# Attention with soft experts on one core: x transposed into the products' bank, the second head's maxima transposed at the block's end, another order of the start and of the late weights' tiles

## The chip, the core and the metric

The kernel runs on one core of a Trainium2 chip. The metric is the device time of one execution in microseconds. The core has a matrix engine (TensorE, PE; its weight loads run in a queue of their own, PEld), three engines for elementwise work (VectorE: DVE, ScalarE: ACT, GpSimd: POOL), and SyncE (SP), which here only issues DMA transfers. Every engine takes its instructions in program order; between engines semaphores order the work.

## The reference

Attention with a causal mask over 8 batches of 12 heads, then a soft mixture of experts over the whole output. All is float32.

```
q, k, v: 8 x 12 x 448 x 64
scores = (q @ k^T) / sqrt(64), above the diagonal -1e9
attn = softmax(scores);  o = attn @ v
x = o as 3584 rows x 768
logits = x @ phi                       # phi 768 x 32: 8 experts x 4 slots
d = softmax(logits over rows)          # dispatch weights
slots = d^T @ x                        # 32 x 768
out_e = relu(slots_e @ w1_e) @ w2_e    # w1 768 x 1024, w2 1024 x 768, 8 experts
c = softmax(logits over slots)         # combine weights
result = c @ out
```

## The kernel before, in words

**Blocks.** The 96 heads are taken in 48 pairs; `block(p)` handles pair p, with heads a = 2p and a + 1, six blocks to a batch. The blocks overlap: block p computes the first part of the scores of the heads a + 2 and a + 3 and finishes those of a and a + 1.

**Scores.** q and k are split in a rounded part (`qd`, `ks`, cast by ACT) and the rest (POOL's subtractions `sub_q`, `sub_k`; `r2_`, named `r20` and `r21`, holds q's rest). `scores1_all` puts the mask and the product of the rounded parts in one of three score tiles `s_`, each two PSUM banks. `max_keys` is DVE's maximum over keys: one pass over the tile with a transposition (1.25 us), then two small ones, into `r_`. `max_row` transposes these maxima on PE (`rt`) and reduces them once more on DVE (`mr`, negated). `max_spread`, a select on POOL, writes them into r2_, from where `scores2` adds them, with the products of the rests, to the scores by matmul. `exps` is ACT's exponential (`pt`).

**Products.** `attv` and `attv3` multiply pt by v (`va`) into `po`, a PSUM bank for both heads. The v tile has a column of ones, so po holds the sums of the exponentials too. `norm(p, 0..2)` divides by them on DVE: sums (`sm`), reciprocals, then x, in one tensor operation and two small ones. `xtrans(p)` transposes x on PE (`xt`, four matmuls), and ACT copies it out (`xts`).

**PSUM.** The three score tiles take six banks, po one, and the last one is the buffer "m" that `misc` gives out in turn: to rt, to xt and to filler matmuls (`warm`).

**The mixture.** With xt of two blocks, `next_logits` adds a third of a batch's logits (PE into a score tile, DVE into `lt`). Which work stands at the end of block p follows from m6 = p % 6: at 2, 4 and 0 logits, at 0 also the batch's maximum (`logits_b`), at 1 the dispatch weights' transposes (`logits_e`), at 3 and 5 a `dispatch`, eight matmuls of x with the dispatch weights, added to `si` on DVE. The last block carries the second dispatch of the batch before the last. After block 47 come the last logits, and the experts, whose weights are 64 pieces of 768 KB, some loaded two at a time.

**Loads.** SP issues all loads of q, k, v and weights in one queue, in program order; one that waits holds all behind it. w0 to w22 have space of their own and are loaded in every second block (`load_w`). The others, w23 to w34, called the late loads here, lie over tiles of attention, in the order in which these were allocated (the pools raw, `fix`, `wk`, `moe`); each waits for the last reader of what it overwrites. `hw`, the next load, waits for a matmul of the first expert.

**Order.** Nothing is scheduled by the compiler: the helper `_InOrder.call` (L65, the line of all instructions in the profile) keeps the order in which the code is written. `START` holds the counts of filler matmuls in the prologue. `later` is a list of small settings on POOL (mk, run_m, run_z, si, sid, srep), of which blocks 1 to 6 issue two each.

Of the kernel before, what the change touches and what calls it, by code (L numbers as in the profile page):

```python
# [17 lines left out]
P = 128  # L18
# [17 lines left out]
HT = 2  # L36
WN, PAD = 1536, 168
WARM = (2, 5, 2, 3, 3)
START = (8, 3, 5, 1, 18, 9)


FILL = 9
# [38 lines left out]
def attention_soft_moe(ctx: ExitStack, tc: tile.TileContext, qk, va, phi, w1, w2, out):  # L81
# [16 lines left out]

    x_, va_, pt_ = [None] * XB, [None, None], [None, None]
    qd_, ks_ = [fix.tile([P, 2, S], F32R, name="qd0")], [fix.tile([P, 2 * S + KP], F32R, name="ks0")]  # L100
    x_[1] = fix.tile([P, NCH, 3 * P], F32, name="x1")
    qd_.append(fix.tile([P, 2, S], F32R, name="qd1"))
    r_ = [fix.tile([P, RW], F32, name=f"r{i}") for i in range(2)]
    ks_.append(fix.tile([P, 2 * S + KP], F32R, name="ks1"))
    r2_ = [fix.tile([P, 2, S], F32R, name="r20")]
    va_[0] = fix.tile([P, NCH, 2, VC], F32, name="va0")

    k2_ = fix.tile([P, 2 * S + KP], F32R, name="k2")
    r2_.append(fix.tile([P, 2, S], F32R, name="r21"))
    pt_[0] = wk.tile([P, 1024], F32, name="pt0")  # L110
# [80 lines left out]
    nc.gpsimd.affine_select(out=tri, in_=tri, compare_op=ALU.is_ge, fill=NEG,  # L191
                            base=0, pattern=[[1, P]], channel_multiplier=-1)

    pob = ps_1.tile([P, NQ * VC], F32, name="po")
    po2 = pob.rearrange("p (a b)->p a b", b=VC)
    po0 = po2[:, 0:NCH]
    identb = const.tile([P, P], BF16, name="identb")

# [11 lines left out]
    def misc(name):  # L210
        return ps_1.tile([P, 512], F32, tag="m", name=name)
# [37 lines left out]
    def scores1(i, part):  # L249
        if i >= NHD:  # L250
            return
        p, h = divmod(i, 2)
        ks, qd = ks_[p % NR], qd_[p % NR]
        if ("s", i) not in st:
            st["s", i] = s_[i % 3]
            st["open"] = set()
        s = st["s", i]

        bank = part in ("c12", "k1", "k2")
        start = bank not in st["open"]  # L260
        st["open"].add(bank)
        if part[0] == "k":
            c = int(part[1])
            o, w, m = S * h + P * c, S - CQ0[c], min(P, S - P * c + KP)
            nc.tensor.matmul(s[0:m, SCOL[c]:SCOL[c] + w], ks[:, o:o + m],
                             qd[:, h, CQ0[c]:S], start=start, stop=False, skip_group_check=True)
            return
        if part == "c12":
            o = s[:, SC1:SC1 + 2 * SC2].rearrange("p (a n) -> p a n", n=SC2)[:, :, 0:P]
            mask = tri.unsqueeze(1).to_broadcast([P, 2, P])  # L270
        else:
            w = P if part == "c0" else S - 3 * P
            o, mask = s[:, SCOL[int(part[1])]:SCOL[int(part[1])] + w], tri[:, 0:w]
        nc.tensor.matmul(o, identb, mask, start=start, stop=False, skip_group_check=True)
# [26 lines left out]
    def max_row(i, k):  # L301
        if i >= NHD:
            return
        if k == 0:
            st["rt", i] = misc(f"rt{i}")
            nc.tensor.transpose(out=st["rt", i][0:RW - RF, 0:P], in_=r_[i % 2][:, RF:RW], identity=ident)
        else:
            mr = st["mr", i] = wk.tile([NQB, 32], F32, tag="mr", name=f"mr{i}", bufs=2)
            nc.vector.tensor_reduce(out=mr, in_=st.pop(("rt", i))[0:NQB, 0:P].rearrange("p (g t)->p t g", g=4),
                                    axis=AX.X, op=ALU.max, negate=True)  # L310
# [12 lines left out]
    def scores2(i, cs):  # L323
        if i >= NHD:
            return
        p, h = divmod(i, 2)
        s = st["s", i]
        k2, r2 = k2_, r2_[p % NR]
        for c in cs:
            o, w, m = S * h + P * c, S - CQ0[c], min(P, S - P * c + KP)  # L330
# [55 lines left out]

    def xtrans(p):
        x = st.pop(("x", p))
        pt = misc(f"xt{p}")
        for c in range(NCH):  # L390
            nc.tensor.transpose(out=pt[:, P * c:P * c + P], in_=x[:, c], identity=ident)
        xt = st["xt", p] = xtp.tile([P, 512], F32, tag="xt", name=f"xts{p}", bufs=XT)
        nc.scalar.activation(out=xt, in_=pt, func=AF.Copy)

    def logits_a(b, js, g, first=True, last=True):

# [52 lines left out]
        logits_a(b, (j, j + 1), m[:, 0:P])  # L449
        logits_t(j, m[:, 0:P])  # L450

    warm(START[0], a=x_[1][:, NCH - 1, 0:AW].bitcast(BF16))
    h0, h1 = slice(0, 1), slice(1, 2)
    cast_k(0, h0)
    cast_q(0, h0)
    cast_k(0, h1)
    for hs in (h0, h1):
        sub_k(0, hs, nc.vector)
    sub_q(0, h0)
    scores1_all(0)  # L460
    warm(START[1])

    cast_q(0, h1)
    sub_q(0, h1)
    scores1_all(1)
    warm(START[2])
    copy_k2(0, h0)
    cast_k(1, h0)
    cast_k(1, h1)
    cast_q(1, h0)  # L470
    copy_k2(0, h1)
    cast_q(1, h1)

    for i, k in ((0, 0), (0, 1), (0, 2), (1, 0)):
        max_keys(i, k)
    sub_k(1, h0)
    max_row(0, 0)
    warm(START[5], pob[:, 0:2 * P])
    max_row(0, 1)
    max_spread(0)  # L480
    for k in (1, 2):
        max_keys(1, k)
    sub_k(1, h1, nc.vector)
    cast_k(2)
# [5 lines left out]
    for hf in range(2):  # L490
        nc.sync.dma_start(out=phis[hf], in_=phi[:, 3 * hf:3 * hf + 3])
# [17 lines left out]

    later += [lambda: nc.gpsimd.tensor_copy(out=srep, in_=sid.unsqueeze(1).to_broadcast([P, 4, NSLOT]))]  # L510

    def block(p):
        a, b = 2 * p, p // 6 - 1
        last, m6 = p == NPAIR - 1, p % 6
        if p + 1 < NPAIR:
            loads_v(p + 1, nc.sync if p + 1 < NPAIR - 1 else nc.scalar)
        if p % 2 and p // 2 < RES:
            load_w(p // 2)
        load_qk(p + 3, 0)

        max_row(a + 1, 0)
        max_row(a + 1, 1)
        max_spread(a + 1)
        if p:
            norm(p - 1, 2)
        else:
            sub_q(1)
        scores2(a, range(NCH))
        exps(a)
        scores1_all(a + 2)  # L530
        for k in range(3):
            max_keys(a + 2, k)
        cast_q(p + 2)
        if p:
            xtrans(p - 1)
        scores2(a + 1, range(NCH))
        exps(a + 1)
        scores1_all(a + 3)
        max_keys(a + 3, 0)
        sub_k(p + 2)  # L540
        load_qk(p + 4, 1)
        sub_q(p + 2)
# [6 lines left out]
        max_spread(a + 2)  # L549
        for k in (1, 2):  # L550
# [354 lines left out]
```

## Time and profile before

| | us |
|---|---|
| median of 3 runs (lowest to highest) | 431.97 (431.29 to 433.31) |
| the profiled execution | 431.9 |
| its span in the trace | 430.2 |
| PE busy / DVE busy / ACT busy / POOL busy | 378.6 / 296.9 / 284.1 / 263.6 |
| first products of block 0 | 17.05 |
| products of block 46 | 320.38 |
| issue of hw | 337.98 |
| last matmuls of the experts | 402.52 |

The span runs from the first to the last event of the trace; 1.7 us of the execution lie outside it. In the rows below, the columns are start, duration, engine, line, operation, output<-inputs, partitions x elements and count; brackets give how long the engine stood idle before, and which event ended that. PE's ends overlap, since its matmuls are pipelined.

### The profile page before, as it was taken

How to read it: one execution, taken by the hardware profiler on the slowest of the kernel's cores; microseconds unless marked ns; L12 is line 12 of the kernel's file. 1: busy time of each engine (PE TensorE's matmuls, PEld its weight loads, DVE VectorE, ACT ScalarE, POOL GpSimd, SP SyncE). 2: the span in 40 equal slices, each digit the busy share in tenths (PEclk: the TensorE clock that was granted, in tenths of full speed). 3: DMA queues.
4: the chain of work that ended last, by engine and by line, in shares of the span. 5: the costliest groups of instructions: out<-in, count | busy, mean ns of one | idle time of the engine just before them, and what ended most of it. 6: DMA issues, size and time to landing. Idle time of an engine off the chain costs nothing.

```text
span 430.2 us, 14170 instructions
## 1 busy us (share of the span) xinstructions
PE 378.6 (88%) x5763; PEld 288.9 (67%) x5763; DVE 296.9 (69%) x817; ACT 284.1 (66%) x400; POOL 263.6 (61%) x215
## 2 busy tenths in 40 slices
PE   6799899999999999999999999999998998968740
PEld 3587778777877777787788777777876644533430
DVE  5777687787787877877877878778774575332440
ACT  5587788878877977888788779778863112422340
POOL 5798988878877978888788779787850000000000
PEclk9999999999999999999999999999999999999985
DMA  7668776777767787767777767876575999999998
GB/s 263 218 216 278 238 251 195 263 252 249 261 187 249 257 257 249 249 194 262 255 243 247 230 218 258 257 257 240 161 272 201 418 419 425 423 422 413 401 389 345
DMA packets 34481, 119.18 MB, mean 277 GB/s; under 512 B 3824, under 2 KB 8944, under 8 KB 32880
## 3 DMA queue, kind: packets, MB, share of 16 engines
q1 hardware_dynamic: 34272, 118.01, 77.9%
q8 instruction: 46, 0.75, 0.7%
q10 hardware_dynamic: 144, 0.27, 0.2%
q14 instruction: 19, 0.16, 0.1%
HBM read 107.25 MB, written 11.01 MB: 275 GB/s over the span
## 4 chain that ended last, share of the span: by engine, by line
PE 37%; DVE 27%; DMA 14%; POOL 8%; issue 5%; ACT 1%; DVEq 0%; POOLq 0%; SPq 0%
PE po L65 18%; DMA w<-in_w_dram 14%; DVE r L65 14%; PE s L65 11%; DVE x L65 7%; POOL r L65 5%; PE rt L65 2%; DVE mr L65 2%; POOL ks L65 2%; PE xt L65 1%; PE pp L65 1%; DVE lt L65 1%; PE hp L65 1%; PE e L65 1%; DVE si L65 1%
## 5 line engine op out<-in xcount | busy, mean ns | idle before, releaser
L65 ACT ACTIVATE pt<-s 128x1024 f32<-128x1024 f32 x96 | 98.4, 1025 | 56.5 <-PE s L65 38.1
L65 DVE TRANSPOSE_TENSOR_REDUCE r<-s 128x32 f32<-128x1024 f32 x96 | 120.0, 1250 | 12.5 <-PE s L65 10.3
L65 POOL TENSOR_TENSOR r<-qk,qd 64x896 fp32r<-64x896 f32 (+1 forms) x49 | 101.0, 2061 | 3.8 <-ACT qd L65 3.6
L65 POOL TENSOR_TENSOR ks<-qk,ks 64x896 fp32r<-64x896 f32 (+1 forms) x47 | 97.9, 2084 | 3.7
L65 PE MATMUL po<-va,pt 128*64 128x65 f32 x3040 | 99.4, 223 | 0.0
L65 PEld LDWEIGHTS po<-va,pt 128*64 128x64 f32 x3040 | 92.8, 138 | 5.8 <-issue 0.2
L65 POOL TENSOR_SCALAR_AFFINE_SELECT r<-mr 14x448 fp32r<-14x448 f32 x96 | 61.4, 640 | 52.4 <-DVE mr L65 47.0
L65 PE MATMUL s<-qd,ks 128*66 128x64 f32 (+3 forms) x384 | 79.2, 318 | 1.9 <-DVE ks L65 1.9
L65 PE MATMUL s<-r,k 128*128 128x448 f32 (+3 forms) x384 | 69.3, 302 | 5.1 <-POOL r L65 4.1
L65 PEld LDWEIGHTS s<-r,k 128*128 128x128 f32 (+1 forms) x384 | 58.6, 183 | 9.8 <-POOL r L65 8.3
L65 PEld LDWEIGHTS s<-qd,ks 128*128 128x128 f32 (+1 forms) x384 | 50.6, 184 | 2.1 <-DVE ks L65 2.1
L65 ACT ACTIVATE ks<-qk 128x896 fp32r<-128x896 f32 (+1 forms) x50 | 46.0, 922 | 6.5 <-DMA qk<-in_qk_dram 2.5
L65 ACT ACTIVATE qd<-qk 128x896 fp32r<-128x896 f32 (+1 forms) x50 | 45.8, 915 | 1.3 <-DMA qk<-in_qk_dram 1.3
L65 ACT ACTIVATE k<-ks 64x896 fp32r<-64x896 f32 (+1 forms) x49 | 45.8, 935 | 1.1
L65 PE MATMUL s<-tri,identb 128*128 128x128 bf16 (+2 forms) x288 | 43.2, 238 | 1.2
L65 PE MATMUL rt<-ident,r 128*76 128x128 f32 x96 | 27.7, 288 | 11.9 <-DVE r L65 11.8
L65 DVE TENSOR_REDUCE r<-r 128x16 f32<-128x32 f32 x192 | 33.7, 176 | 4.9
L65 PEld LDWEIGHTS rt<-ident,r 128*76 128x76 f32 x96 | 11.0, 115 | 38.9 <-issue 23.5
L65 PE MATMUL xt<-ident,x 128*128 128x128 f32 x188 | 31.7, 285 | 2.5 <-DVE x L65 2.5
L65 DVE TENSOR_SCALAR sm<-po 128x7 f32<-128x7 f32 (+1 forms) x48 | 7.9, 165 | 35.6 <-PE po L65 35.6
L65 PEld LDWEIGHTS xt<-ident,x 128*128 128x128 f32 x188 | 22.4, 140 | 11.5 <-PE s L65 4.6
L65 PEld LDWEIGHTS <-identb 128*128 128x128 bf16 x320 | 24.9, 100 | 5.5 <-issue 4.5
(137 smaller groups left out, 400.5 us busy)
## 6 DMA issues: line engine op xcount, KB each, us to landing
qk<-in_qk_dram SPq DMA_DIRECT2D x94, 448.0 KB, 4.5
w<-in_w_dram SPq DMA_DIRECT2D x43, 768.0 KB, 6.0
w<-in_w_dram SPq DMA_DIRECT2D x10, 1536.0 KB, 24.9
va<-in_va_dram SPq DMA_DIRECT2D x47, 260.0 KB, 3.5
out_dram<-ot SPq DMA_DIRECT2D x16, 384.0 KB, 6.7
out_dram<-ot SPq DMA_DIRECT2D x2, 1536.0 KB, 9.3
qk<-in_qk_dram SPq DMA_DIRECT2D x4, 224.0 KB, 3.3
hw<-in_w_dram SPq DMA_DIRECT2D x1, 768.0 KB, 12.1
```

The costliest lines, as they stand in the source:

```text
L65: return self._tc.keep_in_program_order(op(*args, **kwargs))
```

## The change

1. `xtrans` writes its four transposes into po's bank (now 512 columns) and not into the buffer "m", and ACT copies from there.
2. `max_row` and `max_spread` of the second head (a + 3) move from the start of the next block to the end of this one, right behind the products; 64 columns are transposed (`AW`) instead of 76.
3. The prologue: 14 filler matmuls in place of 44; head 0 is done alone first, without the `KP` = 2 extra columns of keys, which belong to head 1; `later` is issued at once, behind the first subtraction; one more subtraction on DVE and one more on POOL change places; block 0 takes over some of the casts and subtractions.
4. The `fix` tiles are allocated in another order, so the late loads lie over other tiles.
5. w22 is loaded in block 44 and not in block 45.
6. The dispatch of the last block moves to the end of block 46, into the second bank of its score tile.

```diff
-START = (8, 3, 5, 1, 18, 9)
+START = (8, 4, 2)
...
     qd_, ks_ = [fix.tile([P, 2, S], F32R, name="qd0")], [fix.tile([P, 2 * S + KP], F32R, name="ks0")]
+    r2_ = [fix.tile([P, 2, S], F32R, name="r20")]
+    qd_.append(fix.tile([P, 2, S], F32R, name="qd1"))
+    ks_.append(fix.tile([P, 2 * S + KP], F32R, name="ks1"))
+    va_[0] = fix.tile([P, NCH, 2, VC], F32, name="va0")
     x_[1] = fix.tile([P, NCH, 3 * P], F32, name="x1")
-    qd_.append(fix.tile([P, 2, S], F32R, name="qd1"))
     r_ = [fix.tile([P, RW], F32, name=f"r{i}") for i in range(2)]
-    ks_.append(fix.tile([P, 2 * S + KP], F32R, name="ks1"))
-    r2_ = [fix.tile([P, 2, S], F32R, name="r20")]
-    va_[0] = fix.tile([P, NCH, 2, VC], F32, name="va0")
...
-    pob = ps_1.tile([P, NQ * VC], F32, name="po")
+    pob = ps_1.tile([P, 512], F32, name="po")
...
-            o, w, m = S * h + P * c, S - CQ0[c], min(P, S - P * c + KP)
+            o, w, m = S * h + P * c, S - CQ0[c], min(P, S - P * c + (KP if i else 0))
...
-            nc.tensor.transpose(out=st["rt", i][0:RW - RF, 0:P], in_=r_[i % 2][:, RF:RW], identity=ident)
+            nc.tensor.transpose(out=st["rt", i][0:w, 0:P], in_=r_[i % 2][:, RF:RF + w], identity=ident)
...
     def xtrans(p):
         x = st.pop(("x", p))
-        pt = misc(f"xt{p}")
         for c in range(NCH):
-            nc.tensor.transpose(out=pt[:, P * c:P * c + P], in_=x[:, c], identity=ident)
+            nc.tensor.transpose(out=pob[:, P * c:P * c + P], in_=x[:, c], identity=ident)
         xt = st["xt", p] = xtp.tile([P, 512], F32, tag="xt", name=f"xts{p}", bufs=XT)
-        nc.scalar.activation(out=xt, in_=pt, func=AF.Copy)
+        nc.scalar.activation(out=xt, in_=pob, func=AF.Copy)
...
+    sub_k(0, h0, nc.vector)
+    sub_q(0, h0)
+    for f in later:
+        f()
+    scores1_all(0)
+    warm(START[1])
...
-        if p % 2 and p // 2 < RES:
+        if p % 2 and p // 2 < RES - 1 or p == 2 * RES - 2:
             load_w(p // 2)
...
-        max_row(a + 1, 0)
-        max_row(a + 1, 1)
-        max_spread(a + 1)
         if p:
             norm(p - 1, 2)
...
-            dispatch_a(NB - 2, 1, s_[(a + 2) % 3])
-            dispatch_b(NB - 2, 1, s_[(a + 2) % 3])
...
         attv3(p)
+        max_row(a + 3, 0, AW)
+        max_row(a + 3, 1)
+        max_spread(a + 3)
         for k in range(2):
             norm(p, k)
-        for _ in range(2):
-            if later and p:
-                later.pop(0)()
...
             next_logits(p // 6, m6 - 2, m)
+            if p == NPAIR - 2:
+                dispatch_a(b, 1, m[:, 512:1024])
+                dispatch_b(b, 1, m[:, 512:1024])
```

On DVE at the end of block 2 (a block with logits), before: the sums, then lt, then mr of the second head, then x.

```order
L65 TENSOR_SCALAR sm_507<-po 128x7
L65 RECIPROCAL sm_507<-sm_507 128x7
L65 TENSOR_TENSOR lt<-s_87,mk 128x128
L65 TENSOR_REDUCE mr_527<-rt_525 14x32
L65 TENSOR_TENSOR x_104<-po,sm_507 128x2x3x64
L65 TENSOR_SCALAR x_104<-po,sm_507 64x64 x2
```

And after:

```order
L65 TENSOR_REDUCE mr_514<-rt_512 14x32
L65 TENSOR_SCALAR sm_517<-po 128x7
L65 RECIPROCAL sm_517<-sm_517 128x7
L65 TENSOR_TENSOR lt<-s_87,mk 128x128
L65 TENSOR_TENSOR x_104<-po,sm_517 128x2x3x64
L65 TENSOR_SCALAR x_104<-po,sm_517 64x64 x2
```

mr went from its place before x to the head of the row; its transpose on PE went from behind the logits to ahead of them.

On SP, the late loads w25 to w29 (the names' numbers are the program's), with the engines whose work each waits for; before:

```order
L65 DMA w_5282<-in_w_dram 128x1536 [waits PE_49,Activation_49]
L65 DMA w_5284<-in_w_dram 128x1536 [waits DMAHW6_49,DVE_49,PE_49]
L65 DMA w_5286<-in_w_dram 128x1536 [waits DVE_49]
L65 DMA w_5288<-in_w_dram 128x1536 [waits DVE_49,DMAHW0_49,Activation_49,Pool_49]
L65 DMA w_5290<-in_w_dram 128x1536 [waits DMAHW1_49]
```

And after:

```order
L65 DMA w_5224<-in_w_dram 128x1536 [waits PE_49,Activation_49]
L65 DMA w_5226<-in_w_dram 128x1536 [waits DMAHW6_49,PE_49,Pool_49]
L65 DMA w_5228<-in_w_dram 128x1536 [waits DMAHW7_49,Activation_49]
L65 DMA w_5230<-in_w_dram 128x1536 [waits DMAHW1_49,DVE_49,PE_49]
L65 DMA w_5232<-in_w_dram 128x1536 [waits DVE_49,PE_49]
```

The second of these rows, w26, lies over x1 before, which the last block's dispatch reads; after, it lies over ks0, r20 and qd1, whose last readers are POOL and the first part of the scores of head 95. x1 now lies under w28 and w29.

On POOL, the rows behind the second setting of r2_ in the prologue, before:

```order
L65 TENSOR_TENSOR ks_94<-qk_1_113,ks_94 64x448
L65 AFFINE_SELECT r_95<-mr_212 14x448
L65 AFFINE_SELECT r_95<-mr_235 14x448
L65 TENSOR_TENSOR r_98<-qk_1_115,qd_91 64x896
L65 TENSOR_TENSOR ks_89<-qk_2_118,ks_89 64x896
L65 TENSOR_TENSOR r_95<-qk_2_120,qd_88 64x896
L65 AFFINE_SELECT r_98<-mr_276 14x448
```

And after, behind the settings of `later`:

```order
L65 AFFINE_SELECT r_90<-mr_211 14x448
L65 TENSOR_TENSOR ks_92<-qk_1_113,ks_92 64x448 x2
L65 AFFINE_SELECT r_90<-mr_246 14x448
L65 TENSOR_TENSOR r_98<-qk_1_115,qd_91 64x896
L65 TENSOR_TENSOR ks_89<-qk_2_118,ks_89 64x896
L65 AFFINE_SELECT r_98<-mr_284 14x448
L65 TENSOR_TENSOR r_90<-qk_2_120,qd_88 64x896
```

One more subtraction (of k of pair 1) stands between the first two selects, and the first select of pair 1 (mr_284) now comes before a subtraction for pair 2 instead of after it.

More of the change, by code (lines that the diff above doesn't have):

```diff
@@ L192, in attention_soft_moe @@
                             base=0, pattern=[[1, P]], channel_multiplier=-1)
-    pob = ps_1.tile([P, NQ * VC], F32, name="po")
-    po2 = pob.rearrange("p (a b)->p a b", b=VC)
+    pob = ps_1.tile([P, 512], F32, name="po")
+    po2 = pob[:, 0:NQ * VC].rearrange("p (a b)->p a b", b=VC)
     po0 = po2[:, 0:NCH]
@@ L299, in max_keys, with max_row @@
                                     axis=AX.X, op=ALU.max)
-    def max_row(i, k):
+    def max_row(i, k, w=RW - RF):
         if i >= NHD:
@@ L329, in scores2 @@
         for c in cs:
-            o, w, m = S * h + P * c, S - CQ0[c], min(P, S - P * c + KP)
+            o, w, m = S * h + P * c, S - CQ0[c], min(P, S - P * c + (KP if i else 0))
             nc.tensor.matmul(s[0:m, SCOL[c]:SCOL[c] + w], k2[:, o:o + m],
@@ L450, in next_logits @@
         logits_t(j, m[:, 0:P])
[L452 to L484, printed above, removed]
     sid = const.tile([P, NSLOT], F32, name="sid")
@@ L489, in attention_soft_moe @@
     phis = [const.tile([P, 3, NSLOT], F32, tag="ph", name=f"phi{hf}", bufs=2) for hf in range(2)]
-    for hf in range(2):
-        nc.sync.dma_start(out=phis[hf], in_=phi[:, 3 * hf:3 * hf + 3])
     run_m = [const.tile([P, 1], F32, name=f"run_m{i}") for i in range(2)]
@@ L510, in attention_soft_moe @@
     later += [lambda: nc.gpsimd.tensor_copy(out=srep, in_=sid.unsqueeze(1).to_broadcast([P, 4, NSLOT]))]
+    warm(START[0], a=x_[1][:, NCH - 1, 0:AW].bitcast(BF16))
+    h0, h1 = slice(0, 1), slice(1, 2)
+    cast_k(0, h0)
+    cast_q(0, h0)
+    sub_k(0, h0, nc.vector)
[4 more added lines that the diff above has]
+    warm(START[1])
+    for k in range(3):
+        max_keys(0, k)
+    cast_k(0, h1)
+    cast_q(0, h1)
+    sub_k(0, h1, nc.vector)
+    max_row(0, 0)
+    max_row(0, 1)
+    max_spread(0)
+    warm(START[2])
+    scores1_all(1)
+    sub_q(0, h1, nc.vector)
+    copy_k2(0, h0)
+    cast_k(1, h0)
+    cast_k(1, h1)
+    cast_q(1, h0)
+    sub_k(1, h0)
+    sub_k(1, h1)
+    for k in range(3):
+        max_keys(1, k)
+    for hf in range(2):
+        nc.sync.dma_start(out=phis[hf], in_=phi[:, 3 * hf:3 * hf + 3])
     def block(p):
@@ L516, in block @@
             loads_v(p + 1, nc.sync if p + 1 < NPAIR - 1 else nc.scalar)
-        if p % 2 and p // 2 < RES:
+        if p % 2 and p // 2 < RES - 1 or p == 2 * RES - 2:
             load_w(p // 2)
         load_qk(p + 3, 0)
-        max_row(a + 1, 0)
-        max_row(a + 1, 1)
-        max_spread(a + 1)
         if p:
             norm(p - 1, 2)
-        else:
-            sub_q(1)
         scores2(a, range(NCH))
         exps(a)
+        if p == 0:
+            max_row(1, 0)
+            max_row(1, 1)
+            max_spread(1)
+            copy_k2(0, h1)
+            cast_q(1, h1)
+            sub_q(1)
         scores1_all(a + 2)
@@ L532, in block @@
             max_keys(a + 2, k)
-        cast_q(p + 2)
         if p:
+            cast_q(p + 2)
             xtrans(p - 1)
@@ L537, in block @@
         exps(a + 1)
+        if p == 0:
+            cast_k(2)
+            cast_q(2)
         scores1_all(a + 3)
@@ L541, in block @@
         load_qk(p + 4, 1)
-        sub_q(p + 2)
+        if p:
+            sub_q(p + 2)
         max_row(a + 2, 0)
@@ L549, in block @@
         max_spread(a + 2)
+        if p == 0:
+            sub_q(2)
         for k in (1, 2):
```

## The prediction

> **What bounds the kernel now.** I read the page's head and chain first, then stretches at the end of attention, then one block in order of time.
>
> ```profile
> span 430.2 us, 14170 instructions
> PE 37%; DVE 27%; DMA 14%; POOL 8%; issue 5%; ACT 1%; DVEq 0%; POOLq 0%; SPq 0%
> w<-in_w_dram SPq DMA_DIRECT2D x43, 768.0 KB, 6.0
> hw<-in_w_dram SPq DMA_DIRECT2D x1, 768.0 KB, 12.1
> ```
>
> No single engine bounds the chain: PE and DVE alternate in attention, and the 14% of DMA are its end, the expert weights. The last two rows are transfers of one size, 6.0 us from issue to landing in the median, but 12.1 us for `hw`: about 6.1 us of queue stand ahead of it. Why there is a queue, the stretches and the queue's issues tell (columns of the first: length; busy PE, PEld, DVE, ACT, POOL; granted clock; DMA share; GB/s).
>
> ```profile
> 324.00:329.00 5.00, 4.60 (x82) 3.59 (x82) 1.90 (x9) 2.39 (x3) 0.57 (x2) 1.00 0.19 25
> 329.00:338.00 9.00, 8.06 (x119) 5.52 (x123) 4.64 (x21) 1.83 (x7) 0.00 (x0) 1.00 0.97 399
> 338.00:400.00 62.00, 53.09 (x663) 26.38 (x656) 28.61 (x89) 14.93 (x40) 0.00 (x0) 1.00 1.01 419
> ...
> 315.51 2.28 SPq L65 DMA_DIRECT2D w<-in_w_dram  x3
> 327.63 2.05 SPq L65 DMA_DIRECT2D w<-in_w_dram  x4
> 337.98 0.33 SPq L65 DMA_DIRECT2D hw<-in_w_dram  x1
> ...
> 326.72 0.85 PE L65 MATMUL s<-x,gs 128*32 128x384 f32 x8
> ```
>
> From 338 on DMA runs full, and just before there is a hole of 5 us at 25 GB/s. w23 to w25 go out at 315.51; w26 only at 327.63, just after the dispatch (326.72 + 0.85 = 327.57) that reads x1, the tile whose address w26 takes. All later loads stand behind it on SP.
>
> Now one loop round, a block with logits:
>
> ```profile
> 112.67 0.29 DVE L65 TENSOR_TENSOR lt<-s,mk 128x128 f32<-128x128 f32 x1 [0.26 <-PE s L65]
> 112.88 0.28 DVE L65 TENSOR_REDUCE mr<-rt 14x32 f32<-14x128 f32 x1
> 113.08 0.54 DVE L65 TENSOR_TENSOR x<-po,sm 128x384 f32<-128x384 f32 x1
> 113.28 0.71 PE L65 MATMUL s<-qd,ks 128*128 128x192 f32 x3
> 113.55 0.57 DVE L65 TENSOR_SCALAR x<-po,sm 64x64 f32<-64x64 f32 x2
> 113.82 0.68 PE L65 MATMUL xt<-ident,x 128*128 128x128 f32 x4
> 114.15 1.25 DVE L65 TRANSPOSE_TENSOR_REDUCE r<-s 128x32 f32<-128x1024 f32 x1
> 115.04 0.59 ACT L65 ACTIVATE xts<-xt 128x512 f32<-128x512 f32 x1
> 116.18 2.09 PE L65 MATMUL po<-va,pt 128*64 128x65 f32 x64
> ```
>
> Products (po), then normalization (x), then the maximum (r, 1.25 us), its transpose, the next products. r needs two things that end almost together: x at 113.55 + 0.57 = 114.12 on DVE, and scores1(a+2) at 113.28 + 0.71 = 113.99 on PE; the tail of a semaphore adds about 0.1. So taking work from DVE alone gives nearly nothing here.
>
> **A: prologue and blocks 0 to 6.**
>
> ```profile
> 8.22 1.14 POOL L65 TENSOR_TENSOR r<-qk,qd 64x448 fp32r<-64x448 f32 x1 [2.46 <-ACT qd L65]
> 17.05 0.45 PE L65 MATMUL po<-va,pt 128*64 128x65 f32 x8
> 31.31 2.09 PE L65 MATMUL po<-va,pt 128*64 128x65 f32 x64
> 37.64 2.08 PE L65 MATMUL po<-va,pt 128*64 128x65 f32 x64
> 41.81 0.64 POOL L65 TENSOR_SCALAR_AFFINE_SELECT r<-mr 14x448 fp32r<-14x448 f32 x1
> 44.04 2.09 PE L65 MATMUL po<-va,pt 128*64 128x65 f32 x64
> 51.45 2.09 PE L65 MATMUL po<-va,pt 128*64 128x65 f32 x64
> 57.18 2.09 PE L65 MATMUL po<-va,pt 128*64 128x65 f32 x64
> 64.05 0.45 PE L65 MATMUL po<-va,pt 128*64 128x65 f32 x8
> ```
>
> The first products begin at 17.05; the shorter start should bring them to about 16.2. I carry none of that on: by block 2 POOL's selects and subtractions, of the same number as before, set the pace, so po of block 2 stays at 31.31. Of the setups on POOL (zeroing, and sid's three selects) the largest stand in block 3 between two selects that PE waits for; the second begins only at 41.81. They move to POOL's idle start, 2.46 us ahead of 8.22, which covers them but for some tenths; without that cover they would push the first select, and A's gain would go. Block 3 (37.64 to 44.04, 6.40) falls to the 5.73 of block 5 (51.45 to 57.18): -0.67. Block 4 (44.04 to 51.45, 7.41) falls to the 6.33 of block 2 (31.31 to 37.64), which has logits as well: -1.08. Against that, plain blocks now have the transposed maxima (mr) and their wait ahead of sm: about +0.3 in blocks 3 and 5 each. Block 6, with its logits, gives -0.1 (below). Sum -1.25, taken as **-1.3**; bounds -0.5 (the +0.3 twice as large, little more) and -1.9 (0.6 of the early start survives).
>
> **B: blocks 7 to 46.** mr of the second head moves ahead of sm; its pitch of 0.20 (112.88 to 113.08) leaves the place just before x, but lt still waits for logits, which now stand behind the transpose on PE. x gains at most 0.1, r is held by scores1(a+2): -0.02 in each of 13 logits blocks. In 13 dispatch blocks scores1 waits for the addition to si (0.61, the row at 119.19 below), which mr's new place does not advance: -0.03. In 6 blocks with m6 = 0, DVE alone binds (lt, its maximum, mr, x in one row): 0.20 less the 0.1 by which logits come later, -0.10. In the 7 with m6 = 1, the gain comes over POOL:
>
> ```profile
> 100.59 0.64 POOL L65 TENSOR_SCALAR_AFFINE_SELECT r<-mr 14x448 fp32r<-14x448 f32 x1 [1.28 <-DVE mr L65]
> 106.24 0.59 PEld L65 LDWEIGHTS s<-r,k 128*128 128x128 f32 x4 [0.40 <-POOL r L65]
> 106.21 0.27 ACT L65 ACTIVATE lg<-s 128x128 f32<-128x128 f32 x1
> 107.83 1.25 DVE L65 TRANSPOSE_TENSOR_REDUCE r<-s 128x32 f32<-128x1024 f32 x1 [0.38 <-PE s L65]
> 119.19 0.61 DVE L65 SCALAR_TENSOR_TENSOR si<-si,al,s 128x384 f32<-128x384 f32 x1 [0.47 <-PE s L65]
> ```
>
> POOL's select waits 1.28 for mr; two subtractions later the next select is late and PE waits 0.40. With mr 1.2 earlier that wait goes; next is ACT's copy of the dispatch weights (to 106.48) out of the tile that scores1 takes. r at about 107.65: -0.18. Sum: 6 x 0.10 + 7 x 0.18 + 13 x 0.02 + 13 x 0.03 = **-2.5**.
>
> The new xt transposes write the bank that x reads, and all four now wait for the last x: 114.12 instead of 113.82, so scores2 behind them comes about 0.14 later. Its reader on DVE, the second head's maximum, comes only after the first's 1.25, and xts stands behind ACT's cast until 115.04: covered, I put it at nothing. If that cover fails, 0.14 in 26 logits and dispatch blocks: +3.6. If instead DVE's 0.1 shows in full with little more, -0.12 in them. B runs from -5.0 to +1.7.
>
> The Trainium skill, "PSUM — Partial Sum Buffer", section "PSUM bank collisions raise a hardware error", has it that two engines may not use one bank and quadrant at once, even at other addresses. It speaks against this edit: xt beginning at 113.82 under an x that runs to 114.12, as here, is over. By it the delay is forced in every block; what it costs was priced above without it.
>
> **C: the last block.** The final dispatch moves from block 47 to the end of block 46, ahead of norm(46). There its 0.85 on PE, and 0.61 on DVE, delay x, xt, scores2(95) and the products; in block 47 it stood beside DVE's work for the most part. **+0.85**, the PE time; bounds 0 (all given back in block 47) and 1.2 (half of the DVE time besides).
>
> **D: the late loads.** The tile order makes w26 wait for scores1(95), w27 for ACT's last k copy, w28 for the moved dispatch, w29 to w31 for the last scores and products:
>
> ```profile
> 319.22 0.71 PE L65 MATMUL s<-qd,ks 128*128 128x192 f32 x3
> 320.32 0.95 ACT L65 ACTIVATE k<-ks 64x896 fp32r<-64x896 f32 x1
> 376.44 1.50 PE L65 MATMUL so<-w,ht 128*32 128x384 f32 x16
> 402.52 0.85 PE L65 MATMUL so<-w,hw 128*32 128x384 f32 x8 [0.93 <-DMA w<-in_w_dram]
> ```
>
> On before's clock: w26 at 319.93, w27 321.3, w28 about 324.5, w29 327.3, w30 328.9, w31 330.2, w32 332.8; w33 and w34, which wait for work behind the last products, later by C, at 335 to 336. One takes 786 KB / 419 GB/s = 1.88 us, so they no longer pile up, and hw (337.98 + 0.85) meets an empty queue: **-6.1**, the excess of hw's landing. Bounds: only the hole is filled, 5.00 x (1 - 0.19) = -4.05; or hw lands as by itself, about -7.4. Behind hw only DMA counts (share 1.01): the last expert's matmuls wait for their load. From 376.44 to 402.52 DMA brings seven pairs of loads at 3.7 us; PE's part of a pair is 1.50 and 0.85, some 2.4 with the gaps, 17 us in all. So PE has about 9 us to give before it becomes the bound, more than 6.1.
>
> The sum, -1.3 - 2.5 + 0.85 - 6.1 = -9.05, against the profiled execution: span 421.15, with the 1.7 outside the span 422.85. The runs' median is 0.07 above that execution's 431.9: **422.9 us**.
>
> **Rivals.**
> 1. *Late loads stay late*: w26 or w27 is held by another reader, or the queue in front of hw is refilled elsewhere. For it: SP is one queue, and a single late wait holds all. Against it: the readers named end before 322. Then 431.97 - 1.3 - 2.5 + 0.85 = 429.0.
> 2. *xt's wait reaches the loop*: r and scores1 are within 0.13 of each other, so PE has little room. B = +1.7, 427.1.
> 3. *Slower: products wait for xts.* po now overwrites the bank that ACT copies from. xts ends at 115.63, po begins at 116.18: 0.55 of room. To end slower, 9.1 must be lost in 46 blocks, 0.20 in each, so xts must come 0.75 late; at 0.80 late the kernel takes 422.9 + 46 x 0.25 = 434.4. Against it: xt is only 0.3 later, and ACT's cast covers part.
> 4. *A cold start.* Fewer filler matmuls go ahead of the first scores.
>
> ```profile
> 1.39 3.60 PE L65 MATMUL warm<-x 128*128 128x512 bf16 x8 [1.39 <-DVE x L65]
> 10.71 1.25 PE L65 MATMUL warm<-tri,identb 128*128 128x512 bf16 x5
> ```
>
> Eight take 3.60 at the start (0.45 each), five 1.25 later (0.25): PE speeds up between. If it happens 3 us later, the prologue's scores cost up to 1 us more, POOL starts that much later, and A falls to -0.3: 423.9.
> The Trainium skill, "TensorE: Matmul & The Clock Gate", section "Part 1: The HAM clock gate", says that full rate follows some 3.4 us of sustained work and goes after an idle window. The two rows agree with a switch; where it falls in the new prologue no run shows yet.
>
> **How the numbers follow.** Forecast with its own spread (420.5 to 425.3) 0.64; rival 1 0.10; rival 2 0.10; rival 3 0.04; rival 4 0.05; a gain beyond the forecast (B, D near their lower ends, 415 to 420.5) 0.07. The range 418.5 to 427.7 leaves out rival 1, rival 3 and the lower part of the last, under 0.2. About 0.5% (2.2 us) is what can be told from no change: under 429.8 is faster. Half of rival 1's spread lies above that: same 0.05, slower 0.04, faster 0.91.
>
> **What would show it.** Block 7's products at about 62.8; setup on POOL before 9 us, none between selects at 40; the second select of an m6 = 0 block no longer 1.28 after the first; r in m6 = 1 blocks without PE's wait on POOL; rounds from one po to the next of 6.3 for logits; w26 issued near 316 in place of 327.63; no stretch of 25 GB/s; hw landing after about 6 us, and some 86 us from its issue to the end in place of 92.2. I am wrong if po starts right after an xts copy, if scores2 waits for xt and r for it, or if hw still lands after 10 us or more.

## The result, and the profile after

The changed kernel takes 427.45 us in the median of 4 runs (426.55 to 427.6), the kernel before 432.31 in 4 runs beside it: a ratio of 0.988 (0.986 to 0.991). That is 4.9 us faster, where 9.1 were forecast; the time is inside the range, 0.25 us under its upper end (427.7). The profiled execution took 427.31, its span is 425.4, against 430.2 before.

First the head of the page, the chain, and the two transfers of one size:

```profile
span 425.4 us, 14150 instructions
...
PE 66%; DVE 18%; DMA 4%; issue 2%; ACT 1%; POOL 0%; DVEq 0%
...
w<-in_w_dram SPq DMA_DIRECT2D x43, 768.0 KB, 6.1
...
hw<-in_w_dram SPq DMA_DIRECT2D x1, 768.0 KB, 6.3
```

DMA has gone from 14% of the chain to 4%, POOL from 8% to 0%, and hw lands nearly like the median load. That is not because DMA has become idle: the chain now comes to the last load by way of PE's work, up to 382.7, while the transfers run full as before (share 1.01 from 338 on). The hole in them is gone (columns as in the prediction):

```profile
324.00:329.00 5.00, 3.76 (x77) 3.44 (x75) 2.03 (x9) 2.58 (x3) 0.00 (x0) 1.00 0.94 337
...
338.00:400.00 62.00, 56.48 (x688) 28.25 (x678) 30.25 (x93) 16.16 (x43) 0.00 (x0) 1.00 1.01 416
```

Five rows of the timeline are the stations by which the four terms of the sum can be read off: products of block 0, of block 7 and of block 46, issue of hw, last expert matmuls.

```profile
15.41 2.09 PE L65 MATMUL po<-va,pt 128*64 128x65 f32 x64
62.26 0.34 PE L65 MATMUL po<-va,pt 128*64 128x65 f32 x4
319.30 0.92 PE L65 MATMUL po<-va,pt 128*64 128x65 f32 x24
337.86 0.33 SPq L65 DMA_DIRECT2D hw<-in_w_dram  x1
397.77 0.85 PE L65 MATMUL so<-w,hw 128*32 128x384 f32 x8 [0.95 <-DMA w<-in_w_dram]
```

| stretch | before | after | measured | forecast (bounds) |
|---|---|---|---|---|
| A: start to block 7's products | 64.05 | 62.26 | -1.79 | -1.3 (-1.9 to -0.5) |
| B: block 7 to block 46 | 256.33 | 257.04 | +0.71 | -2.5 (-5.0 to +1.7) |
| C: block 46's products to hw's issue | 17.60 | 18.56 | +0.96 | +0.85 (0 to 1.2) |
| D: hw's issue to the end of the span | 92.22 | 87.54 | -4.68 | -6.1 (-7.4 to -4.05) |
| span | 430.2 | 425.4 | -4.8 | -9.05 |

Each term is within its bounds, which are wide. B has the wrong sign and makes 3.2 of the 4.2 us that are missing, D 1.4. A second profile of the changed kernel (after_again below) has A, B and C again within 0.1 us, but -5.5 in D: the last stretch differs by 0.8 between two executions of one kernel. B as rounds from one block's products to the next: logits 6.31 to 6.39, dispatch 6.83 to 6.87, m6 = 0 6.87 to 6.90, m6 = 1 6.32 to 6.16.

The block with logits that the prediction read, in the changed kernel:

```profile
110.13 0.30 PE L65 MATMUL rt<-ident,r 128*64 128x128 f32 x1
110.36 0.65 PE L65 MATMUL s<-xts,phi 128*32 128x128 f32 x16
110.54 0.28 DVE L65 TENSOR_REDUCE mr<-rt 14x32 f32<-14x128 f32 x1 [0.74 <-PE rt L65]
110.93 0.73 PE L65 MATMUL s<-r,k 128*128 128x448 f32 x4
111.14 0.29 DVE L65 TENSOR_TENSOR lt<-s,mk 128x128 f32<-128x128 f32 x1
111.35 0.55 DVE L65 TENSOR_TENSOR x<-po,sm 128x384 f32<-128x384 f32 x1
111.71 0.71 PE L65 MATMUL s<-qd,ks 128*128 128x192 f32 x3
111.81 0.57 DVE L65 TENSOR_SCALAR x<-po,sm 64x64 f32<-64x64 f32 x2
112.44 0.65 PE L65 MATMUL po<-ident,x 128*128 128x128 f32 x4
112.47 1.25 DVE L65 TRANSPOSE_TENSOR_REDUCE r<-s 128x32 f32<-128x1024 f32 x1
113.47 0.59 ACT L65 ACTIVATE xts<-po 128x512 f32<-128x512 f32 x1
114.50 2.09 PE L65 MATMUL po<-va,pt 128*64 128x65 f32 x64
```

The transposition now stands ahead of the logits, and these start 0.23 behind it (110.13 to 110.36). lt, counted from the block's products (108.11 here, 109.87 before), comes at 3.03 instead of 2.80: just those 0.23. They eat the 0.20 that mr's removal frees, so x starts at 3.24 instead of 3.21; PE's scores1 begins at 3.60 instead of 3.41, and r at 4.36 instead of 4.28. DVE's own row comes to the same point: sm, now behind mr and the wait for it, begins at 2.64 instead of 2.13, and lt follows without a gap. So in a block with logits two delays meet at lt, PE's and DVE's. In a dispatch block PE's shows alone: the addition to si comes at 3.24 instead of 3.01 and still waits 0.22 for PE. xt starts at 112.44, only when the last x ends (112.38), and r does not wait for it.

The step of the forecast that goes over POOL shows as well. The first row is POOL's second select in the block with m6 = 0, the other two are of the block behind it, with m6 = 1:

```profile
97.81 0.64 POOL L65 TENSOR_SCALAR_AFFINE_SELECT r<-mr 14x448 fp32r<-14x448 f32 x1 [0.67 <-DVE sm L65]
104.24 0.72 PE L65 MATMUL s<-r,k 128*128 128x448 f32 x4
106.08 1.25 DVE L65 TRANSPOSE_TENSOR_REDUCE r<-s 128x32 f32<-128x1024 f32 x1
```

The select comes 2.8 us after its block's products (95.04; before 3.9), scores2 in the next block no longer waits for POOL, and r comes there at 4.13 instead of 4.28.

### The profile page after: what moved, and what is told of

Read it like the earlier page. It is cut to its first block, busy times and chain, and to the rows that moved or that the text cites. A ratio compares the mean times of both kernels' runs of the same rounds, so it can differ in the third digit from the quotient of the medians.

```text
span 425.4 us, 14150 instructions
## 1 busy us (share of the span) xinstructions
PE 382.2 (90%) x5752; PEld 288.2 (68%) x5752; DVE 296.9 (70%) x817; ACT 283.6 (67%) x400; POOL 265.8 (62%) x215
## 4 chain that ended last, share of the span: by engine, by line
PE 66%; DVE 18%; DMA 4%; issue 2%; ACT 1%; POOL 0%; DVEq 0%
PE po L65 29%; PE s L65 23%; DVE x L65 7%; PE rt L65 5%; DMA w<-in_w_dram 4%; PE so L65 2%; DVE si L65 2%; PE pp L65 2%; PE hp L65 2%; DVE lm L65 2%; DVE sm L65 1%; DVE mr L65 1%; DVE lg L65 1%; PE cp L65 1%; PE e L65 1%
## 5 line engine op out<-in xcount | busy, mean ns | idle before, releaser
L65 POOL TENSOR_TENSOR r<-qk,qd 64x896 fp32r<-64x896 f32 (+1 forms) x48 | 100.0, 2083 | 11.8 <-ACT qd L65 6.5
L65 POOL TENSOR_TENSOR ks<-qk,ks 64x896 fp32r<-64x896 f32 (+1 forms) x48 | 98.9, 2060 | 4.2 <-ACT ks L65 0.5
L65 PE MATMUL s<-qd,ks 128*128 128x448 f32 (+4 forms) x384 | 78.2, 315 | 0.7 <-POOL ks L65 0.4
L65 PEld LDWEIGHTS s<-r,k 128*128 128x128 f32 (+1 forms) x384 | 55.9, 176 | 19.3 <-issue 12.5
L65 PEld LDWEIGHTS s<-qd,ks 128*128 128x128 f32 (+2 forms) x384 | 49.7, 181 | 1.0 <-POOL ks L65 0.6
L65 DVE TENSOR_REDUCE mr<-rt 14x32 f32<-14x128 f32 x96 | 24.8, 258 | 36.4 <-PE rt L65 36.3
L65 PE MATMUL po<-ident,x 128*128 128x128 f32 x188 | 30.7, 286 | 8.1 <-DVE x L65 6.2
L65 PEld LDWEIGHTS po<-ident,x 128*128 128x128 f32 x188 | 19.8, 140 | 22.5 <-DVE x L65 22.4
L65 ACT ACTIVATE xts<-po 128x512 f32<-128x512 f32 x47 | 27.9, 594 | 2.4 <-PE po L65 1.3
```

The costliest lines, as they stand in the source:

```text
L65: return self._tc.keep_in_program_order(op(*args, **kwargs))
```

## The experiments

Theory 1: the place of the second head's transposition, ahead of the logits, costs PE 0.23 us, and that is B. Its maximum on DVE goes with it in every run that moves it, so the runs test the place of both; how PE and DVE share the cost they do not tell. The rival is the one named in the prediction, with a fitting time (427.1): xt's wait for the last x, which the shared bank forces, reaches the loop. All kernels are the changed one with the edit shown.

**The transposition behind the other work** (rt_behind).

```diff
         attv3(p)
-        max_row(a + 3, 0, AW)
-        max_row(a + 3, 1)
-        max_spread(a + 3)
...
             logits_b(b, lt)
+        max_row(a + 3, 0, AW)
+        max_row(a + 3, 1)
+        max_spread(a + 3)
```

> The changed kernel with the second head's transposition and maximum (max_row, max_spread of a + 3) behind the block's logits or dispatch instead of ahead of them; all else as changed. Theory 1 (the transposition ahead of the logits costs PE 0.23 us there, which lt and si wait for): rounds after block 7 go back to 6.31 (logits), 6.83 (dispatch), 6.87 (m6 = 0) and 6.32 (m6 = 1), block 7 to block 46 takes 256.3 us instead of 257.0, and the plain blocks 3 and 5 fall from 6.15 to about 5.73; the time is about 425.9. Rival (xt waiting for the last x is what costs): rounds stay at 6.39, 6.87, 6.91, those of m6 = 1 go up to 6.32, block 7 to 46 takes about 258.1, the time is about 427.7.

Rounds were 6.30 (logits), 6.83 (dispatch), 6.87 (m6 = 0) and 6.33 (m6 = 1): theory 1's, and not the rival's, though xt still waits for the last x here.

```profile
111.17 0.64 PE L65 MATMUL s<-xts,phi 128*32 128x128 f32 x16
111.74 0.30 PE L65 MATMUL rt<-ident,r 128*64 128x128 f32 x1
111.80 0.72 PE L65 MATMUL s<-r,k 128*128 128x448 f32 x4
111.95 0.29 DVE L65 TENSOR_TENSOR lt<-s,mk 128x128 f32<-128x128 f32 x1 [0.19 <-PE s L65]
113.42 1.25 DVE L65 TRANSPOSE_TENSOR_REDUCE r<-s 128x32 f32<-128x1024 f32 x1
```

Behind the logits the same transposition takes 0.06 of PE (111.74 to 111.80), and lt comes at 2.80 again. The time was a miss: 427.96 (427.86 to 428.2) and not 425.9. Blocks 3 and 5 took 6.33, not 5.73, since PE now waits for POOL there (0.39 in block 5), and block 1 took 7.50 instead of 7.06, so block 7's products come at 62.98 instead of 62.26. Block 7 to 46 came to 256.96: two single rounds were longer (6.67 in block 8, 6.50 in block 28), without which it would be about 256.4. What lengthened them is not known.

**x in a bank of its own again** (xt_own_bank).

```diff
     def xtrans(p):
         x = st.pop(("x", p))
+        pt = misc(f"xt{p}")
...
-            nc.tensor.transpose(out=pob[:, P * c:P * c + P], in_=x[:, c], identity=ident)
+            nc.tensor.transpose(out=pt[:, P * c:P * c + P], in_=x[:, c], identity=ident)
...
-        nc.scalar.activation(out=xt, in_=pob, func=AF.Copy)
+        nc.scalar.activation(out=xt, in_=pt, func=AF.Copy)
```

> The changed kernel with x transposed into the misc bank again instead of the products' bank. Theory 1: r is held by scores1, which stands ahead of xt on PE, so nothing changes in the loop: rounds stay 6.39 (logits), 6.87 (dispatch), 6.91 and 6.16, block 7 to 46 257.0, time 427.4. Rival (xt's wait costs 0.07 a block): logits rounds 6.31, dispatch 6.83, block 7 to 46 about 255.2, time about 425.7.

```profile
111.15 0.65 PE L65 MATMUL s<-xts,phi 128*32 128x128 f32 x16
112.60 0.57 DVE L65 TENSOR_SCALAR x<-po,sm 64x64 f32<-64x64 f32 x2
...
113.06 0.60 PE L65 MATMUL xt<-ident,x 128*128 128x128 f32 x4
113.26 1.25 DVE L65 TRANSPOSE_TENSOR_REDUCE r<-s 128x32 f32<-128x1024 f32 x1
...
326.65 1.38 PE L65 MATMUL po<-va,pt 128*64 128x65 f32 x32
```

xt starts 0.2 ahead of r, under the last x, and yet the rounds are the changed kernel's: 6.39, 6.87, 6.90, 6.15; block 7 to 46 took 256.83. The rival falls. In the last block, though, the own bank counts: block 46's products to block 47's took 6.65 (320.00 to 326.65) instead of 7.26, and 17.97 to hw's issue instead of 18.56. The time was 426.69 (426.27 to 427.05).

**76 columns** (rt_76): `max_row(a + 3, 0)` in place of `max_row(a + 3, 0, AW)`.

> The changed kernel with 76 columns in the second head's transposition, not 64. Theory 1 (its place costs, not its width): rounds stay 6.39, 6.87, 6.91, 6.16; time 427.4. Rival (the narrow transposition is what makes the next matmuls wait): the 0.23 between the transposition and the logits falls to about 0.06 and logits rounds to 6.31.

```profile
110.66 0.31 PE L65 MATMUL rt<-ident,r 128*76 128x128 f32 x1
110.89 0.65 PE L65 MATMUL s<-xts,phi 128*32 128x128 f32 x16
```

Again 0.23, and the rounds stay at 6.39 and 6.88: the place counts, the width does not. The time is of one run only, 428.66.

**The end undone** (late_undone): the old order of the `fix` tiles, w22 in block 45, the last dispatch in block 47.

> The changed kernel with the old order of the fix tiles, w22 in block 45 and the last dispatch in block 47 again. If the late loads' gain is the 2.0 MB that they put ahead of hw's issue (4.75 us at 419 GB/s) and the moved dispatch costs 0.96: w26 goes out at about 326.5, hw lands after about 12 us, 64.5 us from hw's issue to the last expert matmuls, time 427.45 + 4.75 - 0.96 = 431.2. If the loads are worth the 6.1 of the forecast and something in the changed kernel's end took 1.4 back: time about 432.6.

```profile
327.21 0.80 SPq L65 DMA_DIRECT2D w<-in_w_dram  x2
```

```profile
hw<-in_w_dram SPq DMA_DIRECT2D x1, 768.0 KB, 12.4
```

The first row is the issue of w26 and w27 on SP, the second hw's way from issue to landing. w26 is held to 327.21, hw lands after 12.4, and from its issue (337.54) to the span's end (430.0) it takes 92.5, as before. The time is 432.09 (431.67 to 432.67), between the two that were expected, and the kernel before took 432.10 on the same chip (ratio 0.999, 0.997 to 1.002). So nearly the whole gain of the change is the late loads': A's 1.7 in this run is taken back by B (0.6) and by what is left of C (0.6), all but 0.4. C went down by 0.34 only (18.22), so the moved dispatch is a third of C; x's own bank, two runs above, has the rest.

**Which half of it** (tiles_old: the old order of the tiles alone; dispatch_last: the dispatch in block 47 alone).

> The changed kernel with the old order of the fix tiles alone; w22 stays in block 44 and the last dispatch at the end of block 46. w26 then lies over x1 again and goes out behind that dispatch, at about 323.6 instead of 319.2. If the order of the tiles makes the gain: DMA lies idle for 4 us before it, hw lands after about 9 us or more, time 429 or more. If the moved dispatch makes most of it: the later loads catch up until 334, hw lands after 6 to 7.5 us, time 427.4 to 428.3.

> The changed kernel with the last dispatch in block 47 again; the new order of the tiles and w22 in block 44 stay. w26 and w27 go out at about 319 and 321 as changed, w28 (over x1) only behind that dispatch at about 326.5. From block 46's products to hw's issue 18.2 us instead of 18.6. If most of the late loads' gain is the moved dispatch: hw lands after 8 us or more, from hw's issue to the end 89 us or more, against 87.5 as changed and 92.5 with both undone. If the order of the tiles does it: about 87.5.

```profile
324.42 1.49 SPq L65 DMA_DIRECT2D w<-in_w_dram  x3
```

```profile
hw<-in_w_dram SPq DMA_DIRECT2D x1, 768.0 KB, 8.6
```

```profile
327.21 0.33 SPq L65 DMA_DIRECT2D w<-in_w_dram  x1
```

```profile
hw<-in_w_dram SPq DMA_DIRECT2D x1, 768.0 KB, 8.9
```

The first two rows are of tiles_old (w26 held), the others of dispatch_last (w28 held): an issue on SP, and how long hw took from issue to landing. hw to the end took 88.5 (427.2 - 338.68) and 88.4 (426.0 - 337.56), between the branches of what was expected. Either edit alone brings some 4.0 of the 92.5; both together 5.0 (5.8 in after_again). They aren't added, it seems because each alone lets enough loads go before 327. w22 stays in block 44 in both runs; what that edit brings was not tested alone. Times 428.47 (428.42 to 428.9) and 428.36 (427.75 to 428.74).

**Output writes held back** (outs_held): the writes of the output's first half go out behind the first write of the second.

```diff
-        if k < FILL:
+        if k < FILL and hf == 0:
+            held.append((ov[:, :, sl], ot[:, :, sl]))
+        elif k < FILL:
             nc.sync.dma_start(out=ov[:, :, sl], in_=ot[:, :, sl])
+            while held:
+                o, i = held.pop(0)
+                nc.sync.dma_start(out=o, in_=i)
...
```

> The changed kernel with the writes of the output's first half issued only after the first write of the second half, behind the last weights. If 0.35 to 1 MB of output writes among the weights took back part of the late loads' gain: from hw's issue to the last expert matmuls 57.5 us instead of 59.9 (0.99 MB at 419 GB/s); the time 425.1 if the end is bound by its chain of matmuls and copies, 427.4 if it is bound by the writes. If the writes do not delay the weights: 59.9 and 427.4 or more.

This was to tell what took 1.2 us of D: hw lands 5.8 earlier (12.1 to 6.3), the last expert matmuls, counted from hw's issue, only 4.6 (64.54 to 59.91). What DMA moved between these two events, first before, then after:

```profile
DMA packets 3828, 26.98 MB, mean 418 GB/s; under 512 B 402, under 2 KB 833, under 8 KB 2541
```

```profile
DMA packets 3640, 24.98 MB, mean 417 GB/s; under 512 B 369, under 2 KB 1029, under 8 KB 2353
```

That is 2.00 MB less, 4.8 us at 418 GB/s, but the sum mixes two things. The packets between 512 B and 2 KB are writes of the output: 660 instead of 431. Those between 2 and 8 KB are loads of 6144 B each: 1324 instead of 1708, which is 2.36 MB or 5.6 us less, near the 5.8 of hw's landing.

The writes aren't what took the 1.2: without them among the weights the last matmuls still come 59.7 after hw's issue, while DMA stands idle:

```profile
396.00:400.00 4.00, 3.06 (x25) 1.27 (x26) 1.20 (x4) 0.61 (x3) 0.00 (x0) 1.00 0.04 17
...
420.00:433.00 13.00, 0.00 (x0) 0.00 (x0) 0.00 (x0) 0.00 (x0) 0.00 (x0) 0.50 0.93 380
```

The kernel takes 435.73 (435.04 to 437.04): held writes cost 8 us, since after the matmuls nothing but writes is left and DMA is busy to the last. What the 1.2 is, the second profile of the changed kernel shows (after_again; hw is issued at 337.99 there and lands after 7.1):

```profile
397.09 0.85 PE L65 MATMUL so<-w,hw 128*32 128x384 f32 x8 [0.88 <-DMA w<-in_w_dram]
```

Here hw lands 5.0 earlier than before and the last matmuls come 5.4 earlier (59.10 after its issue). In the nine profiles of kernels that have the end of the changed one, writes included, hw lands after 6.3 to 7.5 (median 7.1), and the way to the last matmuls takes 59.1 to 60.7 (median 59.7): 5.0 and 4.8 less than before (late_undone, with the old end, has 12.4 and 64.76). So the gap of 1.2 belongs to the one execution, not to the change. Why the last loads come later in some executions stays open.

**The settings back in the blocks** (later_old): `later` is issued two by two in blocks 1 to 6, as before the change.

> The changed kernel with the settings of later issued two per block in blocks 1 to 6 again. If they are what made blocks 3 and 4 long: block 3 stays near 6.4, block 4 near 7.4, and block 7's products come at about 63.5 to 63.9 instead of 62.3 (a cold start of PE, which adds up to 0.9, set apart by the first products' time); time about 428.8. If the shorter start alone makes the gain: block 7 at 62.3 to 62.6, time 427.5.

```profile
47.83 0.74 PE L65 MATMUL s<-r,k 128*128 128x448 f32 x4 [1.51 <-POOL r L65]
52.26 0.92 PE L65 MATMUL po<-va,pt 128*64 128x65 f32 x24
```

Block 4 takes 8.83 (43.43 to 52.26), with 1.51 and 0.96 of waiting for POOL's selects; block 7's products come at 65.90, 3.55 later than in the unchanged kernel on the same chip (62.35), 0.56 of which stands already at the first products (16.09 and 15.53). Block 5 takes 6.73; block 3 stays at 6.16, where 6.4 was expected. So the settings between POOL's selects do make blocks long, though not block 3, and dearer than expected: without the move of `later` the changed kernel reaches block 7 some 3 us later. Time 430.33 (429.78 to 430.92).

**Two better orders.** mixed puts the transposition first where m6 = 1 and in blocks 0, 3 and 5, and behind the other work elsewhere:

```diff
+        first = m6 == 1 or p in (0, 3, 5)
+        if first:
+            max_row(a + 3, 0, AW)
...
+        if not first:
+            max_row(a + 3, 0, AW)
...
```

> The changed kernel with the second head's transposition and maximum ahead of the block's other work only in blocks with m6 = 1 and in blocks 0, 3 and 5, and behind logits and dispatch in all others. Theory 1 (the transposition ahead of logits costs PE 0.23 there; ahead of logits_e it lets POOL's select go early): rounds 6.30 (logits), 6.83 (dispatch), 6.87 (m6 = 0), 6.16 (m6 = 1), block 7 to 46 about 255.2 us against 257.0 as changed; time about 425.6. If instead the two orders disturb each other from block to block (POOL's second select is late again in the block behind): rounds of m6 = 1 go to 6.33 and the time to about 427.

> The same with x transposed into the misc bank again. In the loop nothing changes (rounds as in the kernel before this one). In the last block the products no longer wait for xts: from block 46's products to block 47's 6.65 instead of 7.26; time about 425.0. Rival (the products' bank gains something in the loop, since rt and xt no longer share a buffer): rounds longer than in the kernel before this one, time 426 or more.

Rounds were 6.30, 6.83, 6.87, but 6.33 at m6 = 1, as in the second branch of what was expected: the transposition was put first in the wrong block. The select that POOL waits for is that of the block before, m6 = 0, so PE still waits for POOL:

```profile
104.61 0.62 PE L65 MATMUL s<-r,k 128*128 128x448 f32 x2 [0.17 <-POOL r L65]
```

Times 427.10 (426.24 to 427.57; block 42 alone took 7.22 in the profile, it is not known why), and with x in the misc bank (mixed_own) 426.44 (426.0 to 427.05), with 6.61 to block 47's products. With `first = m6 == 0` and x in the misc bank (m0_first_own), against the changed kernel again (after_again):

> The changed kernel with the second head's transposition and maximum ahead of the block's other work only where m6 = 0, behind it in all other blocks, and x transposed into the misc bank. In the run before, rounds of m6 = 1 stayed at 6.33 although the transposition stood first in those blocks; so what makes them short is its place in the block before, m6 = 0, whose maximum POOL's select waits for. Expected: rounds 6.30 (logits), 6.83 (dispatch), 6.90 (m6 = 0), 6.16 (m6 = 1), block 7 to 46 about 255.3 us, block 46 to 47 6.6; time about 425.4, 1.0 under the kernel without this. If the place in the block itself counts after all: rounds of m6 = 1 stay at 6.33, time 426.4.

> The changed kernel itself, unchanged, on the same chip as the three others. All theories: rounds as before, block 7 to 46 257.0. The first products come at 15.4 to 16.4, by when PE gets fast in the prologue; time 427.4, or up to 0.9 more where it gets fast late.

```profile
96.71 1.41 POOL L65 TENSOR_SCALAR_AFFINE_SELECT r<-mr 14x448 fp32r<-14x448 f32 x2
103.94 0.72 PE L65 MATMUL s<-r,k 128*128 128x448 f32 x4
105.60 1.25 DVE L65 TRANSPOSE_TENSOR_REDUCE r<-s 128x32 f32<-128x1024 f32 x1
```

POOL's two selects follow each other without a gap, r comes at 3.99 in the block with m6 = 1, whose round is 6.02 (logits 6.30, dispatch 6.83, m6 = 0 6.91). That is 0.14 less than in the changed kernel, since in this block too the transposition no longer stands ahead of the other work. Block 7 to 46 takes 254.40 instead of 257.08. The time is 424.05 (423.84 to 425.3), a ratio of 0.980 (0.977 to 0.982) to the kernel before; the changed kernel took 427.76 (426.41 to 428.14) on the same chip, 0.987 (0.984 to 0.990). This version beats both, by 1.4 more than expected.

## Why the prediction was right and wrong

**A, right in the main, by luck so near.** The settings leave blocks 3 and 4, and block 7 comes at 62.26 (forecast 62.8); that they held block 4 later_old confirms, that they held block 3 it does not. The plain blocks cost 0.43 (5.73 to 6.16 in block 5), not 0.3, and blocks 2 to 6 together brought 0.74 instead of 1.25. But 1.05 of the early start survived to block 2's products (30.26 instead of 31.31), which the sum had set at nothing and the lower bound at 0.6. How much of that is chance of the clock (last section) is not known: the kernel before, in its one profile, was still slow at 8.22, with three filler matmuls in 1.50.

**B, wrong, by one step.** "0.20 less the 0.1 by which logits come later": the transposition's cost ahead of the logits was taken from between the rows, 0.1, and is 0.23; and it was set against x only at m6 = 0. In logits and dispatch blocks it was counted as nothing, on the ground that r hangs on scores1; but scores1 stands behind the transposition as well. On DVE, mr and the wait for it ahead of sm were priced in A for the plain blocks (0.3) and left out in B, where they hold lt too. Forecast per round -0.02, -0.03, -0.10; measured +0.08, +0.04, +0.03. The part over POOL came out as forecast (-0.18; measured -0.16), but as two terms: POOL's alone is -0.30 (6.32 to 6.02 in m0_first_own), and the transposition ahead of that block's own work takes 0.14 back. With the transposition behind the other work, all of them go back. The neighbouring rows had the answer half: the transposition's own 0.30 was in the trace, its pitch at the new place in none.

**Rival 2, right time, wrong reason.** 427.1 was its time, 427.45 the kernel's; xt's wait is there in every block, but costs nothing in the loop, as xt_own_bank shows. "Covered, I put it at nothing" held, for the reason given there.

The Trainium skill, "PSUM — Partial Sum Buffer", section "PSUM bank collisions raise a hardware error", has the two engines keep off one bank. The traces agree in what the change does: in the products' bank xt starts at 112.44, behind x's end at 112.38, and in its own bank at 113.06, while x runs to 113.17. The price was nought in the loop and 0.6 in the last block.

**Rival 3, in one block.** The products wait for xts in block 47 alone (0.22), where x is late and nothing covers it. That and xt's wait there make 0.6 of C's 0.96; the dispatch makes 0.34, not the 0.85 of PE time. **C** came so near its forecast by luck: of its two terms the forecast had one, and that too large.

**D, right mechanism, too large.** w26 goes out at 319.25 rather than behind the last dispatch, so rival 1 did not come (the "near 316" of the last part, 3.8 earlier than 319.9, took for granted the gains of A and B). The mis-sized term is hw's excess landing, 6.1, the whole way down to the median load's 6.0. hw came down to 7.1 in the median of nine profiles, 5.0 less, and the last matmuls follow it with 4.8; in the first profile it was 5.8 and 4.6. PE, as the forecast had it, did not become the bound: it still waits 0.95 for the last load. Its room was smaller than the 9 us of the forecast, though: its waits for loads between 338 and 404 sum to 7.3 before and to 2.9 now.

**Rival 4** is no separate case but a spread over the runs; see the last section.

## What to carry to other kernels

Price a moved instruction at its new place, by the pitch (from its start to the start of what follows) to its new neighbours: the same transposition took 0.06 of PE behind the logits and 0.23 ahead of them, and what waits for the neighbour pays. Take the price of a queue from several executions: the gain at hw's landing and at the last matmuls was 5.8 and 4.6 in the first profile, 5.0 and 4.8 in the median of nine; and when bytes are counted for it, count only those that stand ahead. When a rival's time fits, test its mechanism; here the rival fitted within 0.4 us and was false.

## What the runs showed of the hardware that was not expected

PE's pitch from a transposition to the next matmuls differs with what these are. It was 0.23 where they have weights of 128*32 (logits and dispatch), 0.06 to 0.14 where they have 128*128, whether 64 or 76 columns were transposed. Whether the weights' width is the reason was not tested.

The prologue's clock differs from profile to profile. These rows are of two kernels with the same prologue, the changed one and xt_own_bank:

```profile
5.63 1.04 PE L65 MATMUL warm<-tri,identb 128*128 128x512 bf16 x4
```

```profile
6.17 1.39 PE L65 MATMUL warm<-tri,identb 128*128 128x512 bf16 x4
```

The second is still slow at 6.17, and it becomes slow once more: its granted clock is 0.50 from 14 to 17 us, where the changed kernel has 1.00.

```profile
14.00:17.00 3.00, 3.00 (x24) 2.42 (x25) 1.72 (x4) 2.12 (x3) 1.94 (x2) 0.50 0.63 211
```

Its first products come at 16.38 instead of 15.41, and block 7's at 63.17 instead of 62.26. In the ten further profiles with this prologue the first products came between 15.27 and 15.53, but for one at 16.41 (tiles_old), which has the same second slow stretch. Other runs on these two chips have none, so it looks like chance; no kernel was profiled both ways. If it is, A carries up to 0.9 us of chance, rival 4's size. The Trainium skill, "TensorE: Matmul & The Clock Gate", section "Part 1: The HAM clock gate", says that the window which releases the clock runs freely, so the switch falls differently from run to run; these rows agree with that.
